# K of the next head asked for behind tiles 4 and 5 of a head in place of behind tiles 8 and 9

## The chip, the cores and the metric

The kernel runs on one core of one Trainium2 chip. A core has five engines that run side by side and meet through semaphores: TensorE (PE, matrix products; PEld is its weight load), VectorE (DVE), ScalarE (ACT), GpSimd (POOL) and SyncE (SP). SP computes nothing here: it issues DMA transfers, one after the other in the order of its program, and the transfers run on 16 DMA engines. The metric is device time in microseconds (us), from one launch of the whole kernel. Lower is better.

## The reference

A transformer block with conditioning: a modulated layer norm, attention against a cached K and V, and an MLP-like mixer. In bfloat16, cut to what matters here:

```python
x: (1, 2048, 640); k_cache, v_cache: (1, 32, 2048, 128); wq: (640, 4096); wo: (4096, 640)
h = _layernorm(x) * (1 + ca) + sa
q = (h @ wq).reshape(1, 2048, 32, 128).transpose(0, 2, 1, 3)
scores = einsum('bhqd,bhkd->bhqk', q, k_cache) * 128 ** -0.5
o = einsum('bhqk,bhkd->bhqd', softmax(scores), v_cache)
x = x + ga * (o.transpose(0, 2, 1, 3).reshape(1, 2048, 4096) @ wo)
h = _layernorm(x) * (1 + cb) + sb
x = x + gb * mixer_and_mlp(h)          # w1, w2, w3, w4
```

There are 32 heads of 128 channels, 2048 queries and 2048 keys a head. K and V of one head are 512 KB each.

## The kernel before

**Stages.** A short first stage loads x and the weights and makes the modulated layer norm. Attention follows, from some 35 us to some 1290 us. After it come the product with wo, the mixer and the MLP, to the end. The change is in attention.

**Tiles.** Attention walks over 512 steps `s`: head `h = s // 16`, tile `j = s % 16` of 128 queries. A step does this:

- TensorE makes the scores of the tile, 128 x 2048, in two halves of 1024 (`qk`, L297), from the tile of Q and the transposed K of the head. K is held in two buffers, one for even and one for odd heads.
- VectorE takes each half out of PSUM, negates and scales it into `negS` (three buffers) and reduces it to the maximum of the row (L570). GpSimd joins the two maxima (L580).
- ScalarE makes the exponential into `Pb` (L583), a ring of `RPB = 8` tiles.
- The tile of probabilities has to be transposed before it can meet V. For 14 of 16 tiles this is done by a DMA transpose, a pair of tiles at a time (`transpose`, L234), into `PTs`, a ring of `RPT = 12` tiles. Tiles 10 and 11 are transposed by TensorE in place of it (L264), and taken out of PSUM by ScalarE and VectorE (L273, L275).
- Some steps later (`PVD = 11`) TensorE multiplies the transposed tile with V (`pv`, L310). V has a column of ones beside it, so the sum of the row comes along. ScalarE takes the result out (L561), GpSimd divides by the sum (L451, L458) and stores to a scratch in DRAM by its own queue (L465).
- Between these, TensorE makes Q of the next head in pieces (L248), and ScalarE takes it out (L255).

**What sets the order.** The loops over `s` append operations to one list for each engine, and each engine works its own list in that order. `G.dma("sync", ...)` appends a transfer to SP's list. Waits are worked out from what an operation reads and writes: a transpose waits for the exponential of its second tile, an exponential waits until the transpose of eight tiles earlier has landed, since it takes its place in the ring, and the scores of a head's first tile wait for the landing of K. A wait in SP's list holds everything behind it.

**SP's list in one head.** In order: transposes of pairs (0,1), (2,3), (4,5), (6,7), (8,9); then, at `j == PVD`, which is tile 11, the loads of K and V of the next head, and in every fourth head a block of wo (640 KB, four heads' rows); then the transposes of (12,13) and (14,15). K is loaded by a DMA transpose from DRAM (`load_k`, L207), V by a plain load (`load_v`, L226), wo by a plain load (`load_wo`, L217). K of heads 0 and 1 is loaded before attention starts, so 30 loads of K are in the loop, in heads 1 to 30.

Of the kernel before, what the change touches and what calls it, by code (L numbers as in the profile page):

```python
# [115 lines left out]
def bass_adaLN_cond__mha_block_cached__mixer_s_mlp__prompt_kernel(  # L116
# [3 lines left out]
    _, H, SK, DH = A_k_cache.shape  # L120
# [17 lines left out]
    with ExitStack() as es:  # L138
# [11 lines left out]
        if True:  # L150
            with ExitStack() as es1:
# [53 lines left out]
                def load_k(h):  # L205
                    hb = h % 2
                    G.dma("sync", lambda e: e.dma_start_transpose(KTs[:, hb], A_k_cache[0, h]), ("k", hb), w=[("KT", hb)])  # L207
# [24 lines left out]
                def transpose(g, n):  # L232
                    b, t = g % RPB, g % RPT
                    G.dma("sync", lambda e: e.dma_start_transpose(  # L234
                        PTs[:, t:t + n].rearrange("p r k q -> p (r k) q"), ring[:, b:b + n].rearrange("p r s -> p (r s)")),
                        ("t", b), r=[("Pb", b + i) for i in range(n)], w=[("PT", t + i, z) for i in range(n) for z in range(2)])
# [9 lines left out]
                def q_piece(h, cc, q):  # L246
                    jb = bank(("q", h, cc))
                    G.op("tensor", lambda t: t.matmul(JB[jb], wqg[:, h // WG, q, (h % WG) * 128:(h % WG + 1) * 128], hT[:, q, cc * 512:(cc + 1) * 512],  # L248
                                                      start=(q == 0), stop=(q == KT - 1)),
                         r=[("wq", h), ("hT", cc, q)], w=[("J", jb)])  # L250
# [39 lines left out]
                def qk(s, half):  # L290
                    h, j = divmod(s, NQT)
                    hb = h % 2

                    def f(t):
                        for c2 in range(2):
                            col = half * 1024 + c2 * 512
                            ins = t.matmul(Sps[:, col:col + 512], QT[:, hb, j * 128:(j + 1) * 128],  # L297
                                           KTs[:, hb, col:col + 512], start=True, stop=True)
                        return ins
                    G.op("tensor", f, r=[("QT", hb, j // 4), ("KT", hb)],  # L300
                         w=[("S", half)] + ([("Sb", 2 * half), ("Sb", 2 * half + 1)] if s == 0 else []))
# [110 lines left out]
                def q_head0(cc):  # L412
                    for q in range(KT):
                        q_piece(0, cc, q)
                    q_evac(0, cc)
# [22 lines left out]
                def mod_rows(i):  # L438
                    n0, n1 = MROW[i]
                    bank = PO[:, (i % 2) * 512:(i % 2) * 512 + n1 - n0]  # L440

                    def f(t):
                        for k in range(KT):
                            ins = t.matmul(bank, s_bc[:, k, :], wmodr[:, k, n0:n1], start=(k == 0), stop=(k == KT - 1))
                        return ins
                    G.op("tensor", f, r=[("sbc", k) for k in range(KT)] + [("wm", 1)] + WRK, w=[("O", i % 2)])
                    G.op("scalar", lambda a: a.copy(mod_bc[:, n0:n1], bank), r=[("O", i % 2)], w=[("mod", i)])
# [79 lines left out]
                for s in range(at[-1] + LAG + 1):  # L527
                    h, j = divmod(s, NQT)
                    pvs = PVS.get(s, [])
                    evacs = []  # L530
                    if s <= 2:
                        for i in ((0,), (1, 2), range(3, len(MROW)))[s]:
                            mod_rows(i)
                    if s == 3:
                        G.op("gpsimd", lambda g: g.tensor_scalar(
                            out=mod_bc[:, 2 * D:3 * D], in0=mod_bc[:, 2 * D:3 * D], scalar1=1.0, scalar2=1.0, op0=ALU.add, op1=ALU.mult),
                            r=[("mod", i) for i in range(len(MROW))], w=["mod"])
                    for half in range(2):
                        if s < NG:
                            qk(s, half)  # L540
                        for g_ in pvs:
                            if len(pvs) == 1:
                                pv(g_, half)
                            elif g_ == pvs[half]:
                                pv(g_, 0)
                                pv(g_, 1)
                        if s == 0 and half == 1:
                            q_head0(NQC - 1)
                        if h + 1 < H and 2 * j + half in QPIECE:
                            cc, q = QPIECE[2 * j + half]  # L550
                            q_piece(h + 1, cc, q)
                            if q == KT - 1:
                                evacs.append((q_evac, h + 1, cc))
                        for r, pt in [(r, pt) for r in range(2) for pt in PE_TILES]:
                            g = s - PE_LAG[pt] - r
                            if 0 <= g < NG and g % NQT == pt:
                                t_piece(g, r, half)
                                if half == 1:
                                    evacs.append((t_evac, g, r))
                    for p in [g_ // 2 for g_ in pvs if g_ % 2 == 1]:  # L560
                        G.op("scalar", lambda a, p=p: a.copy(  # L561
                            Of[:, p % 4].rearrange("p z d -> p (z d)")[:, 0:259], PO[:, (p % 2) * 512:(p % 2) * 512 + 259]),
                            r=[("O", p % 2)], w=[("Of", p % 4)])
                    for fn, x, y in evacs:
                        if fn is q_evac or not by_dve(x, y):
                            fn(x, y)
                    for half in range(2):
                        if s < NG:
                            r8 = s % 8
                            G.op("vector", lambda v, half=half, s=s, r8=r8: v.tensor_scalar(  # L570
                                out=negS[:, s % 3, half * 1024:(half + 1) * 1024],
                                in0=Sps[:, half * 1024:(half + 1) * 1024],
                                scalar1=-SCALE, scalar2=None, op0=ALU.mult, op1=ALU.min,
                                accum_out=(nm0 if half == 0 else nm1)[:, r8:r8 + 1]),
                                r=[("S", half)], w=[("negS", s % 3), ("nmh", half, r8)])
                    for fn, x, y in evacs:
                        if fn is t_evac and by_dve(x, y):
                            fn(x, y)
                    if s < NG:
                        G.op("gpsimd", lambda g, r8=r8: g.tensor_scalar(  # L580
                            out=nm[:, r8:r8 + 1], in0=nm0[:, r8:r8 + 1], scalar1=nm1[:, r8:r8 + 1], scalar2=None, op0=ALU.min),
                            r=[("nmh", 0, r8), ("nmh", 1, r8)], w=[("nm", r8)])
                        G.op("scalar", lambda a, s=s, r8=r8: a.activation(  # L583
                            Pb[:, s % RPB, :], negS[:, s % 3, :], ACT.Exp, bias=nm[:, r8:r8 + 1], scale=-1.0),
                            r=[("negS", s % 3), ("nm", r8)], w=[("Pb", s % RPB)])
                        if not is_pe(s):
                            if s % 2 == 1 and not is_pe(s - 1):
                                transpose(s - 1, 2)
                            elif s % 2 == 1 or is_pe(s + 1):
                                transpose(s, 1)  # L590
                        if j == PVD:
                            if 1 <= h < H - 1:
                                load_k(h + 1)
                            if h < H - 1:
                                load_v(h + 1)
                            if h % WG == WG - 1:
                                load_wo(h // WG)
                    for g_ in NORMS.get(s, []):
                        gr, z = divmod(g_, 4)
                        if z == 0:  # L600
                            rcp(gr)
                        norm(gr, z)
                    if s == OT0:
                        load_ot(0)
                        for cc in range(NQC):
                            load_xt(cc)
                    if s == OT0 + 1:
                        load_ot(1)
# [247 lines left out]
```

## Time and profile before

| | |
|---|---|
| time, median of 3 runs | 1629.96 us (1628.02 to 1634.95) |
| profiled execution, its own time | 1635.84 us |
| its span, first to last instruction | 1634.0 us |
| TensorE (PE) busy | 1498.6 us, 92% |
| VectorE (DVE) busy | 1393.1 us, 85% |
| ScalarE (ACT) busy | 1295.6 us, 79% |
| GpSimd (POOL) busy | 622.8 us, 38% |
| loads of K | 32, median 4.7 us from issue to landing |
| transposes of pairs | 224, median 7.4 us from issue to landing |

The profile gives busy time of the engines, idle time and what ended it, and the rows of every instruction. For TensorE, busy time includes pipelined instructions that overlap, so a share of 92% is not 92% of its peak. SP does no work that counts as busy; its rows are the issues of transfers, and a row is as long as the issue takes, with a full queue longer than with an empty one. A row that ends in square brackets tells how long the engine sat idle before it, and whose work ended that.

### The profile page before, as it was taken

How to read it: one execution, taken by the hardware profiler on the slowest of the kernel's cores; microseconds unless marked ns; L12 is line 12 of the kernel's file. 1: busy time of each engine (PE TensorE's matmuls, PEld its weight loads, DVE VectorE, ACT ScalarE, POOL GpSimd, SP SyncE). 2: the span in 40 equal slices, each digit the busy share in tenths (PEclk: the TensorE clock that was granted, in tenths of full speed). 3: DMA queues.
4: the chain of work that ended last, by engine and by line, in shares of the span. 5: the costliest groups of instructions: out<-in, count | busy, mean ns of one | idle time of the engine just before them, and what ended most of it. 6: DMA issues, size and time to landing. Idle time of an engine off the chain costs nothing.

```text
span 1634.0 us, 34765 instructions
## 1 busy us (share of the span) xinstructions
PE 1498.6 (92%) x13978; PEld 978.8 (60%) x14231; DVE 1393.1 (85%) x2460; ACT 1295.6 (79%) x1145; POOL 622.8 (38%) x1394
## 2 busy tenths in 40 slices
PE   5899989998999899989989989999899799999998
PEld 3466666665666566666666666666666555545444
DVE  6999989998999899989999999999899346666424
ACT  4999989998999899989999999999899500045330
POOL 0144444443444344444444444444344423322000
PEclk9999999999999999999999999999999899999999
DMA  9999999999999999999999999999999995530000
GB/s 300 226 233 230 238 242 226 246 229 234 230 239 234 226 240 242 231 232 233 235 229 241 221 234 247 233 232 236 233 228 243 233 217 113 103 110 1 17 16 33
DMA packets 1151730, 333.61 MB, mean 204 GB/s; under 512 B 1127184, under 2 KB 1145552, under 8 KB 1151568
## 3 DMA queue, kind: packets, MB, share of 16 engines
q1 hardware_dynamic: 1145424, 314.58, 96.8%
q0 software_dynamic: 6144, 16.79, 3.9%
q8 instruction: 112, 1.84, 0.5%
q14 instruction: 50, 0.41, 0.1%
HBM read 43.48 MB, written 19.40 MB: 38 GB/s over the span
## 4 chain that ended last, share of the span: by engine, by line
DVE 36%; PE 25%; ACT 19%; issue 12%; DMA 7%; POOL 1%; SPq 1%; POOLq 0%
DVE negS L570 34%; ACT ring L583 13%; PE Sps L643 7%; DMA kv<-in_A_k_cache_dram 4%; PE Sps L784 4%; PE Sps L297 3%; PE PTp L310 2%; ACT Of L561 2%; PE Oaug L768 2%; PE QPp L768 2%; ACT ring L273 2%; ACT kv L255 1%; PE Sps L753 1%; DMA ring<-in_A_x_dram 1%; DVE ring L375 1%
## 5 line engine op out<-in xcount | busy, mean ns | idle before, releaser
L570 DVE TENSOR_SCALAR_CACHE_REDUCE negS<-Sps 128x1024 f32<-128x1024 f32 x1024 | 1177.8, 1219 | 54.4 <-PE Sps L297 51.9
L583 ACT ACTIVATE ring<-negS,small 128x2048 bf16<-128x2048 f32 x512 | 1023.1, 2020 | 16.6 <-POOL small L580 15.6
L310 PEld LDWEIGHTS PTp<-kv,ring 128*128 128x128 bf16 x8192 | 566.6, 99 | 249.1 <-issue 10.4
L297 PE MATMUL Sps<-kv 128*128 128x512 bf16 x1948 | 600.8, 386 | 92.4 <-DMA kv<-in_A_k_cache_dram 51.7
L310 PE MATMUL PTp<-kv,ring 128*128 128x129 bf16 x8192 | 652.5, 222 | 6.0 <-DMA ring<-ring 4.2
L580 POOL TENSOR_SCALAR small<-small 128x1 f32<-128x1 f32 x512 | 145.9, 285 | 654.6 <-DVE negS L570 654.5
L297 PEld LDWEIGHTS Sps<-kv 128*128 128x128 bf16 x2048 | 137.5, 98 | 208.2 <-DVE negS L570 117.8
L458 POOL TENSOR_SCALAR On<-Of,small 128x128 bf16<-128x128 f32 x512 | 189.8, 371 | 13.0
L681 ACT COPY kv<-PTp 128x640 bf16<-128x640 bf16 x32 | 22.0, 692 | 154.6 <-PE PTp L678 154.6
L451 POOL TENSOR_TENSOR small<-Of,small 128x4 f32<-128x4 f32 x128 | 133.1, 1040 | 5.3 <-ACT Of L561 5.2
L561 ACT COPY Of<-PTp 128x259 f32<-128x259 f32 x256 | 96.3, 376 | 40.2 <-PE PTp L310 40.2
L465 POOL DMA_DIRECT2D o_scratch<-On x128 | 103.1, 806 | 40.8 <-POOL On L458 37.2
L248 PE MATMUL Oaug<-hTx,wo 128*128 128x512 bf16 x264 | 100.4, 385 | 3.8 <-DVE hTx L407 3.7
L248 PE MATMUL QPp<-hTx,wo 128*128 128x512 bf16 x260 | 98.1, 382 | 2.7 <-ACT hTx L402 2.2
L570 DVE DVE_READ_ACCUMULATOR negS<-Sps 128x1 f32 x1024 | 84.4, 82 | 0.0
L624 POOL TENSOR_SCALAR On<-On 128x1 f32<-128x1 f32 x48 | 24.3, 507 | 153.0 <-DVE On L633 153.0
L651 DVE TENSOR_TENSOR ring<-Sps,mod_bc 128x640 f32<-128x640 f32 x16 | 13.2, 824 | 76.0 <-PE Sps L643 76.0
L643 PE MATMUL Sps<-wo,hTx 128*128 128x128 bf16 (+1 forms) x504 | 70.9, 302 | 4.7 <-DMA hTx<-o_scratch 4.4
L643 PE MATMUL Sps<-wo,negS 128*128 128x128 bf16 (+1 forms) x504 | 69.1, 298 | 2.1 <-DMA negS<-o_scratch 1.8
L788 DVE TENSOR_TENSOR ring<-Sps,ring 128x640 f32<-128x640 f32 x16 | 13.2, 824 | 66.2 <-PE Sps L784 66.2
L273 ACT COPY ring<-Oaug 128x1024 bf16<-128x1024 bf16 x64 | 64.1, 1001 | 0.0
L643 PEld LDWEIGHTS Sps<-wo,hTx 128*128 128x128 bf16 x512 | 40.0, 99 | 36.0 <-DMA hTx<-o_scratch 4.2
(82 smaller groups left out, 1013.9 us busy)
## 6 DMA issues: line engine op xcount, KB each, us to landing
kv<-in_A_v_cache_dram SPq DMA_DIRECT2D x32, 512.0 KB, 5.1
o_scratch<-On POOLq DMA_DIRECT2D x128, 128.0 KB, 4.8
ring<-in_A_x_dram SPq DMA_DIRECT2D x8, 640.0 KB, 4.9
wo<-in_A_wo_dram SPq DMA_DIRECT2D x8, 640.0 KB, 7.9
wo<-in_A_wq_dram SPq DMA_DIRECT2D x7, 640.0 KB, 8.6
ring<-ring SPq DMA_TRANSPOSE x224, 7.4
ring<-in_w_mod_dram SPq DMA_DIRECT2D x1, 3200.0 KB, 13.7
out_dram<-wo SPq DMA_DIRECT2D x16, 160.0 KB, 1.8
```

The costliest lines, as they stand in the source:

```text
L248: G.op("tensor", lambda t: t.matmul(JB[jb], wqg[:, h // WG, q, (h % WG) * 128:(h % WG + 1) * 128], hT[:, q, cc * 512:(cc + 1) * 512], star ...
L273: G.op("scalar", lambda a: a.copy(dst, src), r=[("J", jb)], w=[("PT", g % RPT, r)])
L297: ins = t.matmul(Sps[:, col:col + 512], QT[:, hb, j * 128:(j + 1) * 128], KTs[:, hb, col:col + 512], start=True, stop=True)
L310: ins = t.matmul(ob[:, 0:129], PTs[:, b, kt, :], Vaug[:, hb, kt, 0:129], start=(kt == 0), stop=(kt == NKT - 1))
L451: G.op("gpsimd", lambda g: g.tensor_tensor(out=rl[:, 4 * b:4 * b + 4], in0=Of[:].rearrange("p a z d -> p (a z) d")[:, 4 * b:4 * b + 4, 128 ...
L458: G.op("gpsimd", lambda g: g.tensor_scalar(out=On[:, b, z, :], in0=Of[:, 2 * b + z // 2, z % 2, 0:128], scalar1=rl[:, 4 * b + z:4 * b + z ...
L465: G.dma("gpsimd", lambda e: e.dma_start(o_scr[jj // 2:jj // 2 + 2, :, hh].rearrange("a p z d -> p a (z d)"), On[:, b].rearrange("p (a z) d ...
L561: G.op("scalar", lambda a, p=p: a.copy(Of[:, p % 4].rearrange("p z d -> p (z d)")[:, 0:259], PO[:, (p % 2) * 512:(p % 2) * 512 + 259]), r= ...
L570: G.op("vector", lambda v, half=half, s=s, r8=r8: v.tensor_scalar(out=negS[:, s % 3, half * 1024:(half + 1) * 1024], in0=Sps[:, half * 102 ...
L580: G.op("gpsimd", lambda g, r8=r8: g.tensor_scalar(out=nm[:, r8:r8 + 1], in0=nm0[:, r8:r8 + 1], scalar1=nm1[:, r8:r8 + 1], scalar2=None, op ...
L583: G.op("scalar", lambda a, s=s, r8=r8: a.activation(Pb[:, s % RPB, :], negS[:, s % 3, :], ACT.Exp, bias=nm[:, r8:r8 + 1], scale=-1.0), r=[ ...
L643: ins = t.matmul(YB[b][:, c0:c0 + cw], OTj[pr % 2][:, 2 * hh + z, :], wo[:, hh, c0:c0 + cw], start=(hh == 0), stop=(hh == H - 1))
```

## The change

The request for K of the next head moves up in SP's list, from behind the transposes of tiles 8 and 9 to behind those of tiles 4 and 5. It is now made at tile 5. The requests for V and for the block of wo stay at tile 11. No instruction is added or taken away.

```diff
                             elif s % 2 == 1 or is_pe(s + 1):
                                 transpose(s, 1)
+                        if j == 5 and 1 <= h < H - 1:
+                            load_k(h + 1)
                         if j == PVD:
-                            if 1 <= h < H - 1:
-                                load_k(h + 1)
                             if h < H - 1:
                                 load_v(h + 1)
                             if h % WG == WG - 1:
```

SP's list in one head is now: (0,1), (2,3), (4,5), K, (6,7), (8,9), V, in every fourth head wo, (12,13), (14,15).

## The prediction

> **What bounds the kernel now.** I read the page first, then the waits of the attention stage, then the busy time head by head, then the SP queue's rows one by one.
>
> ```profile
> span 1634.0 us, 34765 instructions
> q1 hardware_dynamic: 1145424, 314.58, 96.8%
> ```
>
> The span is 1634.0 us; the run that was profiled took 1635.84 us, 1.84 us more than its span, and stands 5.9 us (0.36%) above the median of the three runs, 1629.96. The queue that SP and the transposes use keeps the 16 DMA engines occupied for 96.8% of the span, although its traffic is thin in the last eighth.
>
> The waits between 100 and 1260 us, nearly all of attention (who waited for whom; total, times, longest):
>
> ```profile
> PE Sps L297 <- DMA kv<-in_A_k_cache_dram: 51.7, 21, 5.4
> DVE negS L570 <- PE Sps L297: 47.8, 33, 5.0
> ACT ring L583 <- POOL small L580: 10.8, 28, 1.0
> ```
>
> TensorE waits for K (L297 is the score product), and VectorE, which reduces the scores (L570), waits 47.8 us for TensorE. Nothing else stops VectorE there. Busy time for four successive heads, cut where VectorE starts a head:
>
> ```profile
> 501.32:543.60 42.28, 36.02 (x369) 24.80 (x373) 37.31 (x66) 39.91 (x33) 18.99 (x43) 0.97 1.21 234
> 543.60:582.78 39.18, 37.28 (x369) 26.16 (x375) 37.43 (x65) 35.12 (x30) 15.77 (x37) 0.95 1.17 223
> 582.78:620.01 37.23, 35.96 (x374) 24.98 (x379) 37.23 (x68) 37.20 (x32) 17.43 (x40) 1.00 1.23 247
> 620.01:657.23 37.22, 35.62 (x369) 24.16 (x374) 37.22 (x68) 37.22 (x33) 17.44 (x40) 1.00 1.17 242
> ```
>
> Columns: length, then busy PE, PEld, DVE, ACT, POOL, the clock granted, DMA share, GB/s. An undisturbed head takes 37.22 us, all of it VectorE work: that is VectorE's floor. ScalarE is as full. The first two heads lose 5.0 and 2.0 us. How a large stall looks (VectorE, then TensorE):
>
> ```profile
> 537.40 1.22 DVE L570 TENSOR_SCALAR_CACHE_REDUCE negS<-Sps 128x1024 f32<-128x1024 f32 x1
> 543.60 1.22 DVE L570 TENSOR_SCALAR_CACHE_REDUCE negS<-Sps 128x1024 f32<-128x1024 f32 x1 [4.97 <-PE Sps L297]
> 545.75 1.22 DVE L570 TENSOR_SCALAR_CACHE_REDUCE negS<-Sps 128x1024 f32<-128x1024 f32 x1 [0.92 <-PE Sps L297]
> 547.81 1.22 DVE L570 TENSOR_SCALAR_CACHE_REDUCE negS<-Sps 128x1024 f32<-128x1024 f32 x1 [0.83 <-PE Sps L297]
> 542.53 1.03 PE L297 MATMUL Sps<-kv 128*128 128x512 bf16 x2 [5.43 <-DMA kv<-in_A_k_cache_dram]
> ```
>
> 4.97 us until K lands, then 0.92 and 0.83 us more while TensorE runs below full clock (0.95 over that head) after its 5.43 us of idling. Why K is late stands in the SP queue's own rows:
>
> ```profile
> 458.61 2.35 SPq L207 DMA_TRANSPOSE kv<-in_A_k_cache_dram  x1
> 461.63 33.74 SPq L234 DMA_TRANSPOSE ring<-ring  x7
> 495.41 3.11 SPq L207 DMA_TRANSPOSE kv<-in_A_k_cache_dram  x1
> 498.57 0.58 SPq L226 DMA_DIRECT2D kv<-in_A_v_cache_dram  x1
> 499.19 1.38 SPq L217 DMA_DIRECT2D wo<-in_A_wo_dram  x1
> 500.62 37.16 SPq L234 DMA_TRANSPOSE ring<-ring  x7
> 537.82 2.29 SPq L207 DMA_TRANSPOSE kv<-in_A_k_cache_dram  x1
> 540.78 35.47 SPq L234 DMA_TRANSPOSE ring<-ring  x7
> 576.29 3.54 SPq L207 DMA_TRANSPOSE kv<-in_A_k_cache_dram  x1
> 613.92 2.02 SPq L207 DMA_TRANSPOSE kv<-in_A_k_cache_dram  x1
> ```
>
> SP issues without a break from 458.61 to 537.82: seven pair transposes (L234) of 4 to 8 us each, K, V, and every fourth head a block of wo, all in one line. K at 537.82 stands behind pair (8,9), which itself went out late because everything before it did. So the queue, not the place of K alone, is near its limit. Where SP is not behind, gaps appear between its rows; these are single rows from the one stretch of this cycle that has them:
>
> ```profile
> 546.86 4.23 SPq L234 DMA_TRANSPOSE ring<-ring  x1
> 552.62 4.04 SPq L234 DMA_TRANSPOSE ring<-ring  x1
> 557.28 4.09 SPq L234 DMA_TRANSPOSE ring<-ring  x1
> 561.88 3.89 SPq L234 DMA_TRANSPOSE ring<-ring  x1
> 566.37 5.08 SPq L234 DMA_TRANSPOSE ring<-ring  x1
> ```
>
> Each row's end to the next one's start: 552.62 - 551.09 = 1.53, then 0.62, 0.51 and 0.60, together 3.3 us, right after the large stall. (The table of SP's own waits is no help here: it names the last semaphore step before an issue ended, and an issue that is long because the queue is full looks there like a wait for ScalarE.)
>
> **The change part by part.** Thirty K loads (asked for in heads 1 to 30) move from behind pair (8,9) to behind pair (4,5); no instruction is added or removed, and the four compute engines keep their order. Only SP's order changes: K passes two pair transposes.
>
> *The stalls it removes.* K goes out two pair issues earlier. In the head above the pairs are these, and K's landing is the median over its 32 loads:
>
> ```profile
> 527.87 4.32 SPq L234 DMA_TRANSPOSE ring<-ring  x1
> 532.24 5.54 SPq L234 DMA_TRANSPOSE ring<-ring  x1
> DMA to landing us min/median/max: 4.1/4.7/14.4
> ```
>
> 537.82 - 527.87 = 9.9 us earlier, against a largest wait of 5.43. K would land near 527.9 + 4.7 = 532.6, while TensorE wanted it at 542.53 - 5.43 = 537.1. So I cost all waits for K at zero afterwards; what is removed is 47.8 us of VectorE idling, slow-clock part included.
>
> *K itself.* Its buffer was last read in the head before, so it waits for nothing. Nothing is priced for that: the cover is five tiles of 2.3 us (37.22 / 16).
>
> *The two pairs it passes.* (6,7) and (8,9) go out K's 2 to 3.5 us later. Where SP is ahead, as at 552 to 570, this is hidden by the ring of eight exponential tiles. Where SP is behind, it is not. Pair (6,7) of the head above, issued at 527.87, landed 8.4 us later, at 536.3; the exponential that reuses tile 6's buffer is the last but one of that head:
>
> ```profile
> DMA to landing us min/median/max: 8.4/8.4/8.4
> 536.55 2.01 ACT L583 ACTIVATE ring<-negS,small 128x2048 bf16<-128x2048 f32 x1
> ```
>
> Slack 0.3 us. That is what is late next: with the stall for K gone, ScalarE waits for a landing transpose, VectorE then for ScalarE.
>
> *V and wo.* They go out right after (8,9), as K no longer stands between; V's wait for TensorE lies behind work done two tiles earlier, and behind V stands only wo and pair (12,13). I cost it at zero; without that cover it would be at most K's 2 us, in a place where SP has two tiles (10, 11) without a transpose. POOL's queue, which stores the attention output, keeps its order, and K is as large as before wherever it meets those stores: zero.
>
> *The sum.* One cycle of four heads, K row to K row, is 613.92 - 458.61 = 155.3 us. VectorE needs 4 x 37.22 = 148.9, a surplus of 6.4. SP needs 155.3 - 3.3 = 152.0, if a head in which SP is ahead kept its short issues: gain 3.3. But issues are longer when the queue is full: its backlogged heads took 495.41 - 458.61 = 36.8 and, with wo, 537.82 - 495.41 = 42.4, the third 613.92 - 576.29 = 37.6; three at about 37.2 and one at 42.4 make 154.0: gain 1.3. I take the middle, 2.3 us a cycle, since the new order will have SP behind most of the time but not always. Thirty heads are 7.5 cycles: 17 us. Once only, the queue may fall behind from where it stands at 552 to where it stands at 536, which the ring absorbs, about one wo delay (42.4 - 36.8 = 5.6 us, of which part is used today): 3 us. Together 20 us. Ends kept: 7.5 x 1.3 = 10 and 47.8.
>
> The tail after attention is the same work, so 1634.0 - 20 = 1614 for the span, 1615.8 for its run, and 1629.96 - 20 = 1610 for the median.
>
> The Trainium skill, in "Perfetto Trace Analysis", section What "DMA-bound" means, counts as DMA-bound also a kernel whose issuing sequencer is solid DMA slices. By that rule alone no more than SP's gaps can be won: 7.5 x 3.3 = 25 us, 1605. The unbroken rows from 458.61 to 537.82 agree with it.
>
> **The rivals.**
>
> *A. VectorE takes all of it (48 us, 1582).* If SP's issues get shorter once no engine stalls, the attention heads run at 37.22. For it: the rows of 3.9 to 4.1 us after 552; 7 x 4.1 + 2.3 + 0.6 = 31.6 us plus other queues' traffic would fit. Against: 4.3 to 8 us whenever SP is behind, and wo's 5.6 us every fourth head. In "DMA: Bandwidth & Descriptors", section Rules for kernel authors, the Trainium skill advises to issue a DMA early and wait for it late, so that its fixed cost overlaps; that rule would give this rival, if the queue had room.
>
> *B. No change within 0.5% (1622 to 1638, about 1624).* SP is the limit throughout: stalls for K become waits for landing transposes of nearly the same length. For it: 154.0 of 155.3 us by the backlogged rows, and 96.8% on the queue. Against: the gaps of 3.3 us.
>
> *C. Slower: the pairs pay more than K did.* (6,7) and (8,9) are 2 to 3.5 us later just where the slack is 0.3 us. If ScalarE paid 2.0 us for each of the two pairs, in each of the two heads of a cycle that run backlogged, without any later wait growing shorter, that is 8 us against the surplus of 6.4 that goes: 7.5 x 1.6 = 12 us slower, 1642. It decides when the new waits exceed 6.4 us a cycle. Against it: a delay in one queue is paid once, as SP's total work is the same; and V and wo move forward by what the pairs move back.
>
> **How the numbers follow.** 0.5% of 1630 is 8 us, about what a measurement of this kernel can tell from no change. Forecast (SP-bound, 10 to 35 us won) 0.62; A (35 to 48) 0.14; B 0.16; C 0.08. Faster 0.76, same 0.16, slower 0.08. The range leaves out C, and parts of A and B: 1588 to 1625. Predicted 1610.
>
> **What would show it.** Right: no wait of TensorE for K after head 2; VectorE's idling for L297 from 47.8 to under 25 us and no longer at a head's first tile; K rows two transposes earlier, landing 9 us or so before use; new idling of ScalarE at L583, named by a transpose's landing, in the heads after a wo block; SP's rows solid, with fewer than 25 us of gaps; the granted clock at 1.00 through attention. Wrong: heads of 37.2 us throughout (A); ScalarE's new idling as large as VectorE's was (B) or larger (C); K still waited for, if SP falls more than 10 us behind.

## The result, and the profile after

The changed kernel takes 1613.57 us (median of 6 runs, 1607.07 to 1622.23) against 1630.62 us for the kernel before, measured beside it (6 runs, 1628.02 to 1637.57). The ratio is 0.989, with a 95% interval of 0.9856 to 0.9924: faster by 12 to 23 us, a little over 1%. The forecast was 1610, in a range of 1588 to 1625.

The profiled execution took 1614.36 us, its span 1612.6, 21.4 us less than before. From the page:

```profile
span 1612.6 us, 34765 instructions
q1 hardware_dynamic: 1145424, 314.58, 97.3%
L570 DVE TENSOR_SCALAR_CACHE_REDUCE negS<-Sps 128x1024 f32<-128x1024 f32 x1024 | 1177.8, 1220 | 28.8 <-ACT ring L583 15.8
L583 ACT ACTIVATE ring<-negS,small 128x2048 bf16<-128x2048 f32 x512 | 1028.3, 2046 | 30.0 <-DMA ring<-ring 25.0
```

VectorE's score reduction (L570) still sits idle for 28.8 us, but what ends most of that is now ScalarE's exponential (L583), and what ends the exponential's own idling is the landing of a transpose. The waits between 100 and 1260 us, which are the answer to those shown of before:

```profile
ACT ring L583 <- DMA ring<-ring: 25.0, 25, 2.6
DVE negS L570 <- ACT ring L583: 15.8, 20, 2.1
DVE negS L570 <- PE Sps L297: 4.5, 8, 0.9
```

No wait for K is left; it had been 51.7 us. In its place stands a wait that was not in the trace before: ScalarE for the place of a probability tile in the ring of eight. A large case (2.01 us at ScalarE, where the longest is 2.6), in the chain of waits and then at ScalarE and VectorE:

```profile
495.04 12.11 DMA ring<-ring
507.23 1.03 ACT ring L583
508.26 9.07 DMA ring<-ring
```

```profile
507.23 2.00 ACT L583 ACTIVATE ring<-negS,small 128x2048 bf16<-128x2048 f32 x1 [2.01 <-DMA ring<-ring]
509.36 1.23 DVE L570 TENSOR_SCALAR_CACHE_REDUCE negS<-Sps 128x1024 f32<-128x1024 f32 x1 [1.47 <-ACT ring L583]
```

A pair asked for at 495.04 lands 12.1 us later; the exponential that needs its place has waited 2.01 us, and VectorE then 1.47 for the exponential. SP's queue around it:

```profile
481.08 1.89 SPq L207 DMA_TRANSPOSE kv<-in_A_k_cache_dram  x1
483.02 9.77 SPq L234 DMA_TRANSPOSE ring<-ring  x2
492.83 0.72 SPq L226 DMA_DIRECT2D kv<-in_A_v_cache_dram  x1
493.59 1.40 SPq L217 DMA_DIRECT2D wo<-in_A_wo_dram  x1
495.04 27.93 SPq L234 DMA_TRANSPOSE ring<-ring  x5
523.00 1.81 SPq L207 DMA_TRANSPOSE kv<-in_A_k_cache_dram  x1
524.86 10.27 SPq L234 DMA_TRANSPOSE ring<-ring  x2
535.17 0.58 SPq L226 DMA_DIRECT2D kv<-in_A_v_cache_dram  x1
535.80 24.70 SPq L234 DMA_TRANSPOSE ring<-ring  x5
560.54 2.11 SPq L207 DMA_TRANSPOSE kv<-in_A_k_cache_dram  x1
```

K now stands between five pairs and two, and each row begins where the one before ends. (A row of x5 joins five issues and would hide gaps between them; their sum follows below.) The gaps that the kernel before had after a large stall are gone. Busy time of four heads around this place (columns as before: length; busy PE, PEld, DVE, ACT, POOL; clock; DMA share; GB/s):

```profile
491.13:531.59 40.46, 36.18 (x368) 24.29 (x372) 37.57 (x68) 37.03 (x31) 17.51 (x40) 1.00 1.20 224
531.59:572.81 41.22, 37.46 (x370) 25.80 (x375) 37.57 (x68) 39.19 (x33) 17.52 (x40) 0.96 1.25 245
572.81:610.03 37.22, 35.92 (x369) 24.16 (x374) 37.22 (x68) 37.22 (x33) 17.52 (x40) 1.00 1.27 248
610.03:647.25 37.22, 35.62 (x369) 24.17 (x374) 37.22 (x66) 37.22 (x33) 17.51 (x40) 1.00 1.20 241
```

This is the worst place of the run, and it is as bad as the place shown of before; most heads are nearer to VectorE's 37.22. For the mean, take the first and the last of the 30 requests for K in the loop. Before they stand at 108.54 and 1238.2, 29 heads apart:

```profile
108.54 2.00 SPq L207 DMA_TRANSPOSE kv<-in_A_k_cache_dram  x1
L207 SPq DMA_TRANSPOSE kv<-in_A_k_cache_dram x32: 1717/2247/12325, 8.8 to 1238.2; - x32
```

and after at 99.16 and 1207.6:

```profile
99.16 3.00 SPq L207 DMA_TRANSPOSE kv<-in_A_k_cache_dram  x1
L207 SPq DMA_TRANSPOSE kv<-in_A_k_cache_dram x32: 1487/2309/11809, 9.1 to 1207.6; - x32
```

That is 38.95 us a head before and 38.22 after. The difference, 0.73 us, times 29 is 21.2 us: all of the gain lies in attention. SP's single rows say where it comes from. Over these 29 heads the rows add up to 1092.5 us before and 1095.1 after, 2.6 more; the time between them is 37.2 us before and 13.4 after, 23.8 less, and 23.8 - 2.6 = 21.2. Of gaps longer than 0.15 us alone there were 26.8 us, and 1.8 are left. So the change took SP's idle time away and made its issues no shorter.

### The profile page after: what moved, and what is told of

Its sections match the earlier page's. It is cut to its first block, busy times and chain, and to the rows that moved or that the text cites. A ratio compares the mean times of both kernels' runs of the same rounds, so it can differ in the third digit from the quotient of the medians.

```text
span 1612.6 us, 34765 instructions
## 1 busy us (share of the span) xinstructions
PE 1491.7 (93%) x13978; PEld 959.2 (59%) x14231; DVE 1393.1 (86%) x2460; ACT 1287.8 (80%) x1145; POOL 625.5 (39%) x1394
## 4 chain that ended last, share of the span: by engine, by line
ACT 32%; DVE 21%; PE 21%; DMA 15%; issue 11%; SPq 0%; POOL 0%; ACTq 0%; DVEq 0%; POOLq 0%
ACT ring L583 24%; DVE negS L570 19%; DMA ring<-ring 12%; PE Sps L643 8%; PE Sps L784 4%; ACT Of L561 3%; ACT ring L273 2%; ACT kv L255 2%; PE Oaug L768 2%; PE QPp L768 2%; PE Sps L753 1%; PE Sps L297 1%; DMA ring<-in_A_x_dram 1%; PE PTp L310 1%; DMA o_scratch<-On 1%
## 5 line engine op out<-in xcount | busy, mean ns | idle before, releaser
L570 DVE TENSOR_SCALAR_CACHE_REDUCE negS<-Sps 128x1024 f32<-128x1024 f32 x1024 | 1177.8, 1220 | 28.8 <-ACT ring L583 15.8
L583 ACT ACTIVATE ring<-negS,small 128x2048 bf16<-128x2048 f32 x512 | 1028.3, 2046 | 30.0 <-DMA ring<-ring 25.0
L310 PEld LDWEIGHTS PTp<-kv,ring 128*128 128x128 bf16 x8192 | 560.5, 98 | 246.3 <-DMA ring<-ring 9.8
L297 PEld LDWEIGHTS Sps<-kv 128*128 128x128 bf16 x2048 | 125.4, 97 | 192.4 <-DVE negS L570 160.1
L465 POOL DMA_DIRECT2D o_scratch<-On x128 | 103.1, 806 | 40.8 <-POOL On L458 37.2
L561 ACT COPY Of<-PTp 128x259 f32<-128x259 f32 x256 | 104.6, 409 | 11.2 <-PE PTp L310 11.1
L570 DVE DVE_READ_ACCUMULATOR negS<-Sps 128x1 f32 x1024 | 85.0, 83 | 0.0
L651 DVE TENSOR_TENSOR ring<-Sps,mod_bc 128x640 f32<-128x640 f32 x16 | 13.2, 825 | 80.0 <-PE Sps L643 80.0
L788 DVE TENSOR_TENSOR ring<-Sps,ring 128x640 f32<-128x640 f32 x16 | 13.2, 825 | 66.2 <-PE Sps L784 66.2
```

What stands on the lines that cost most here:

```text
L310: ins = t.matmul(ob[:, 0:129], PTs[:, b, kt, :], Vaug[:, hb, kt, 0:129], start=(kt == 0), stop=(kt == NKT - 1))
L465: G.dma("gpsimd", lambda e: e.dma_start(o_scr[jj // 2:jj // 2 + 2, :, hh].rearrange("a p z d -> p a (z d)"), On[:, b].rearrange("p (a z) d ...
L561: G.op("scalar", lambda a, p=p: a.copy(Of[:, p % 4].rearrange("p z d -> p (z d)")[:, 0:259], PO[:, (p % 2) * 512:(p % 2) * 512 + 259]), r= ...
L583: G.op("scalar", lambda a, s=s, r8=r8: a.activation(Pb[:, s % RPB, :], negS[:, s % 3, :], ACT.Exp, bias=nm[:, r8:r8 + 1], scale=-1.0), r=[ ...
```

## The experiments

Three questions were open. Is it really the transfers that hold the changed kernel above VectorE's 37.22 us, and if so the DMA engines or SP's list? What made K late? And does it matter where in the list K stands? All times are medians; the ratio is to the kernel before, run beside it on the same chip, with its 95% interval. Several chips were used, on which the kernel before took 1629.6 to 1635.3 us, so between two rows of the table the ratios compare better than the microseconds.

| kernel | us | ratio to before |
|---|---|---|
| the changed kernel | 1613.6 | 0.989 (0.9856 to 0.9924) |
| stores twice | 1656.9 | 1.0134 (1.0099 to 1.0169) |
| no K in the loop | 1585.8 | 0.970 (0.9667 to 0.9732) |
| no wo blocks, K as changed | 1594.9 | 0.9767 (0.9724 to 0.9811) |
| no wo blocks, K as before | 1599.8 | 0.9796 (0.9758 to 0.9833) |
| V from ScalarE's queue | 1627.2 | 0.996 (0.9938 to 0.9983) |
| K behind tiles 2 and 3 | 1619.0 | 0.9899 (0.9854 to 0.9943) |
| K behind tiles 6 and 7 | 1617.2 | 0.9898 (0.9863 to 0.9933) |
| wo spread, K as changed | 1600.4 | 0.9799 (0.9763 to 0.9835) |
| wo spread, K as before | 1604.7 | 0.9816 (0.9791 to 0.984) |
| wo spread, K behind 6 and 7 | 1609.3 | 0.9854 (0.9825 to 0.9883) |
| wo spread, K in two halves | 1611.6 | 0.9848 (0.9807 to 0.989) |
| wo spread, behind tiles 0 and 1 | 1611.8 | 0.9884 (0.9863 to 0.9906) |

### Are the transfers the limit?

**The stores of the output issued twice**, in the changed kernel; SP's list is as it was (`o_scr2` is a second scratch that nothing reads):

```diff
+                    G.dma("gpsimd", lambda e: e.dma_start(
+                        o_scr2[jj // 2:jj // 2 + 2, :, hh].rearrange("a p z d -> p a (z d)"),
+                        On[:, b].rearrange("p (a z) d -> p a (z d)", a=2)),
+                        ("o2", b), r=[("On", b, z) for z in range(4)], w=[("os2", b)])
```

> The changed kernel with every store of the attention output issued a second time, into a second scratch that nothing reads: 128 more transfers of 128 KB from GpSimd's queue, none in SP's list. If the 16 DMA engines are the limit: the stores take 3.6% of the engines' time now, 58 us, and as much again comes on top: 1650 to 1675 us, ScalarE's waits for landing transposes several times 25 us. If SP's own list of issues is the limit: 1610 to 1625 us.

43 us more than the changed kernel, 40 by the ratios. From the waits between 100 and 1260 us of this kernel (L588 is the exponential; L585, L459 and L452 are GpSimd's), and the issues of SP's transposes (L235 here; duration in ns as min/median/max):

```profile
ACT ring L588 <- DMA ring<-ring: 51.7, 49, 2.5
ACT ring L588 <- POOL small L585: 5.5, 8, 1.4
ACT ring L588 <- POOL On L459: 3.5, 1, 3.5
ACT ring L588 <- POOL small L452: 2.0, 1, 2.0
```
```profile
L235 SPq DMA_TRANSPOSE ring<-ring x224: 3957/4812/7797, 44.3 to 1305.2; - x112
```

ScalarE's wait for transposes doubles from 25.0 us (I had expected several times as much), though nothing was added in front of a transpose in SP's list. GpSimd has these issues on top too, and ScalarE waits 11.0 us for it (1.4 in the changed kernel), but the time does not go there. SP's rows stay solid: its gaps over 0.15 us are 0.8 us in 29 heads, so SP hardly waits for anyone. And the same rows take longer: the transposes 4812 ns in the median against 4502, all of SP's rows 1136.6 us in 29 heads against 1095.1, 41.5 more. So the DMA engines are shared, and the added bytes are paid in time, inside SP's issues.

**No K in the loop:**

```diff
-                        if j == 5 and 1 <= h < H - 1:
+                        if j == 5 and h < 0:
                             load_k(h + 1)
```

> The changed kernel without the 30 loads of K in the loop (heads 2 to 31 use K of heads 0 and 1, so the output is not the reference's). Theory (transfers are the limit): they lose about 2 us a head, 60 us in all, more than the 22 us that VectorE idles: attention falls to VectorE's pace, 37.2 us a head, 1589 to 1595 us, and gaps appear between SP's rows. If something other than transfers holds the changed kernel above VectorE's pace: 1605 us or more.

1585.8 us, 28 less than the changed kernel (31 by the ratios), a little better than expected. VectorE's pace is reached, and gaps stand between SP's rows (here 2.7, and 3.4 us, after V, where SP waits for the exponential of tile 13):

```profile
501.00:538.20 37.20, 36.47 (x375) 24.12 (x373) 37.20 (x66) 37.20 (x32) 17.49 (x41) 1.00 1.12 232
```
```profile
518.26 0.58 SPq L226 DMA_DIRECT2D kv<-in_A_v_cache_dram  x1
521.58 33.24 SPq L234 DMA_TRANSPOSE ring<-ring  x7
554.86 0.58 SPq L226 DMA_DIRECT2D kv<-in_A_v_cache_dram  x1
558.80 24.05 SPq L234 DMA_TRANSPOSE ring<-ring  x5
```

So nothing but transfers holds the changed kernel above VectorE's floor. This run takes away K's bytes and its place in SP's list at once; it is the run with the stores that tells the two apart.

**V requested by ScalarE's queue:**

```diff
-                def load_v(h):
+                def load_v(h, eng="sync"):
...
-                    G.dma("sync", lambda e: e.dma_start(Vaug[:, hb, :, 0:128], A_v_cache[0, h].rearrange("(t p) d -> p t d", p=128)),
+                    G.dma(eng, lambda e: e.dma_start(Vaug[:, hb, :, 0:128], A_v_cache[0, h].rearrange("(t p) d -> p t d", p=128)),
...
-                                load_v(h + 1)
+                                load_v(h + 1, "scalar")
```

> The changed kernel with V requested by ScalarE's queue in place of SP's, at the same tile. If the time that SP's issues take is the limit: SP's list loses about 2 us a head, 60 us in all, and attention falls to ScalarE's pace with some 0.6 us more work a head, about 1600 to 1604 us. If the 16 DMA engines are the limit (they move the same bytes): no gain, 1609 to 1620 us, and SP's other issues become longer by what V's took.

1627.2 us: 14 us slower than the changed kernel (11 by the ratios), against either expectation's size, but on the side of the engines. (The first expectation takes 2 us a head off SP's list. V's row there is 0.58 us, 18 us over 31 heads and not 60; by this too the kernel should have become faster.) SP's list is shorter and its rows stay solid, since the transposes in it become longer, in the median 4668 ns against 4502:

```profile
L234 SPq DMA_TRANSPOSE ring<-ring x224: 3936/4668/9351, 44.8 to 1278.9; - x112
```
```profile
L234 SPq DMA_TRANSPOSE ring<-ring x224: 3966/4502/8157, 44.5 to 1262.1; - x112
```

The first is this kernel, the second the changed one. ScalarE's wait for transposes grows to 41.0 us. ScalarE's own work grows too, by 31 issues of 0.375 us, 11.6 us in all; but SP's gaps over 0.15 us are 1.8 us in 29 heads, so SP hardly waited for ScalarE, and there the transposes' rows grew by 43 us while those of V and wo shrank by 30. V itself lands 7.7 us after its request, in the median, where it took 5.3. That V now runs beside the transposes in place of behind them, and takes from them at a bad moment, would explain the loss; it was not shown.

### What made K late?

**No wo blocks,** in the changed kernel and in the kernel before:

```diff
-                            if h % WG == WG - 1:
-                                load_wo(h // WG)
```

> The kernel before, K still behind tiles 8 and 9, without the loads of wo blocks (output not the reference's). Theory (K came late because the queue ahead of it was late, and a wo block is what makes it late): the large stalls right after wo heads go, some 35 of the 48 us, so about 1595 us. Rival (the place behind tiles 8 and 9 is too late by itself): the waits for K stay above 30 us and the time above 1618 us.

> The changed kernel without the eight loads of wo blocks in attention (the product with wo then uses what stands in that memory, so the output is not the reference's). Theory (the one queue of SP's transfers limits attention in the changed kernel): the queue loses about 5 us of work a block, 40 us in all, more than the 22 us that VectorE still idles in attention, so attention falls to VectorE's pace: about 1592 us, ScalarE's waits for landing transposes under 5 us. Rival (the two pairs that K passes are late by K itself, whatever else is in the queue): at most 5 us faster than the changed kernel, 1608 us or more, and the waits for transposes stay above 18 us.

From the waits between 100 and 1260 us, without wo and K as before:

```profile
PE Sps L297 <- DMA kv<-in_A_k_cache_dram: 29.5, 22, 3.2
DVE negS L570 <- PE Sps L297: 13.2, 17, 2.1
```

and without wo, K as changed:

```profile
ACT ring L583 <- DMA ring<-ring: 5.7, 10, 1.4
```

With K as before, 1599.8 us: without the wo blocks, K behind tiles 8 and 9 comes nearly in time. TensorE's wait for it falls from 51.7 to 29.5 us and, what counts, VectorE's from 47.8 to 13.2. With K as changed, 1594.9 us, and ScalarE's wait for transposes falls from 25.0 to 5.7. The rivals of both fall; that of the kernel before falls by its time, as waits of 29.5 us are only just under the 30 that it named. The move of K is worth about 5 us here, with intervals that overlap, where it is worth 17 with the blocks. Leaving wo out takes away its bytes as well as the burst; the next two runs keep the bytes.

**Wo spread over the heads**, each block but the last as four loads of 160 KB (`load_woq`), one a head from the head on that asked for the block, at the same place beside V. First with K as changed:

```diff
-                            if h % WG == WG - 1:
-                                load_wo(h // WG)
+                            if h == H - 1:
+                                load_wo(h // WG)
+                            elif h >= WG - 1:
+                                load_woq((h + 1) // WG - 1, (h + 1) % WG)
```

> The changed kernel with each wo block of four heads but the last split into four loads of 160 KB, one in each of the next four heads. If the total work of the queue is the limit: no gain beyond 5 us, 1608 to 1618 us, ScalarE's waits for transposes near 25 us, only spread more evenly. If the bursts are the limit (the queue falls behind after each block and the ring of eight tiles is too short for that peak): most of the 22 us of VectorE's idling goes, about 1595 us.

1600.4 us, the fastest kernel here that does all the work. The bytes are the same, so "the total is the limit" was too simple; the burst counts. ScalarE's wait for transposes is 11.3 us. Then the same with K as before:

> K as in the kernel before, behind tiles 8 and 9, with the wo blocks split into four loads over four heads. Theory (the bursts make the queue late, and lateness makes K late): VectorE's idling for K falls from 48 to some 20 us: about 1603 to 1612 us. Rival (the place of K costs by itself): above 1620 us.

```diff
                         if j == PVD:
+                            if 1 <= h < H - 1:
+                                load_k(h + 1)
```

(in the kernel with wo spread, whose request at tile 5 is taken out). 1604.7 us, as the theory had it, and not to be told from 1600.4 by the intervals. Waits of these two between 100 and 1260 us (K as changed, K as before; L302 and L575 are the score product and its reduction in these files, L588 the exponential):

```profile
ACT ring L588 <- DMA ring<-ring: 11.3, 18, 1.4
DVE negS L575 <- PE Sps L302: 5.8, 9, 1.8
```
```profile
PE Sps L302 <- DMA kv<-in_A_k_cache_dram: 33.8, 25, 3.0
DVE negS L575 <- PE Sps L302: 16.5, 19, 2.1
```

Spreading wo alone, with K left where it was, is worth more (about 1.8%) than moving K alone (1.1%).

### Does K's place matter?

**K behind tiles 2 and 3, or 6 and 7**, with wo in whole blocks (here 7; 3 in the other):

```diff
-                        if j == 5 and 1 <= h < H - 1:
+                        if j == 7 and 1 <= h < H - 1:
                             load_k(h + 1)
```

> The changed kernel with K behind tiles 2 and 3. Theory (peaks): a third pair is pushed, (4,5), whose slack in the changed kernel was 0.1 to 2.8 us, so ScalarE's waits grow by some 5 us: 1614 to 1622 us. If only the total of the queue counts: as the changed kernel, 1610 to 1618 us. If K still came late in the changed kernel: faster than 1608 us.

> The changed kernel with K behind tiles 6 and 7 in place of 4 and 5, wo in whole blocks. Theory (what is left is paid where the lateness of the queue peaks: K's 2 to 3 us push pair (6,7) past the ring's slack): K then passes pair (8,9) alone, which had about 1 us more slack than (6,7), so part of the 25 us of ScalarE's waits goes: about 1606 us, if K still lands in time (it goes out some 4 us later). If only the total of the queue counts: 1610 to 1618 us, waits for transposes near 25 us.

Both come out at a ratio of 0.990, the same as the changed kernel within the intervals. I had thought that what is left is paid at the pairs K pushes; by that theory tile 7 would have been faster, and it was not. What differs is who waits. Behind tiles 6 and 7:

```profile
PE Sps L297 <- DMA kv<-in_A_k_cache_dram: 25.8, 16, 3.7
ACT ring L583 <- DMA ring<-ring: 19.7, 19, 2.9
```

K goes out one pair's issue later and is late again, 16 times and by up to 3.7 us; ScalarE waits less for the transposes. So the place behind tiles 4 and 5 has about one pair of margin: there K lands 4.4 us before TensorE first needs it (median of the 30 loads; 1.3 to 8.9), and a pair takes 4.9 us to issue in the mean.

**With wo spread, K behind 6 and 7, and K in two halves**; the first takes the edit above, the second this one, where `load_kh` loads 1024 keys into half of the buffer and each half of the scores waits for its own:

```diff
-                        if j == 5 and 1 <= h < H - 1:
-                            load_k(h + 1)
+                        if j in (5, 7) and 1 <= h < H - 1:
+                            load_kh(h + 1, j // 2 - 2)
```

> Wo spread over the heads and K behind tiles 6 and 7. Theory (peaks): the 11 us of waits that were left with wo spread and K behind tiles 4 and 5 shrink by half, 1593 to 1598 us. If K's place among the pairs does not matter: 1600 us.

> Wo spread over the heads, and K in two halves of 1024 keys, one behind tiles 4 and 5, one behind 6 and 7. If K's 2 to 3 us as one lump cause the waits that are left with wo spread (11 us): 1592 to 1596 us. If only the amount of transfers counts: 1598 to 1604 us, as with K in one piece.

1609.3 and 1611.6 us: both slower than the 1600.4 with K whole behind 4 and 5, against every number expected. The intervals of the three ratios overlap at their ends, so this is likely and not certain. With K behind 6 and 7 it waits for K again, 33.8 us. With the halves, waits for K are 8.2 us and those for transposes 23.8.

**Wo spread, but behind tiles 0 and 1**, away from V:

```diff
+                        if j == 1 and WG <= h:
+                            load_woq(h // WG - 1, h % WG)
```

> Wo spread over the heads with each 160 KB load behind tiles 0 and 1, away from V, K behind tiles 4 and 5. If a load costs the queue most where it meets V and the gap of tiles 10 and 11 (pairs (12,13) then take 6 to 8 us to issue): faster than wo spread beside V, 1592 to 1597 us. If only the amount of transfers counts, with wo in small pieces: 1598 to 1604 us. If the loads use the gap of tiles 10 and 11, in which SP has no transpose to issue, they cost more elsewhere: 1605 to 1612 us.

1611.8 us, the third case: of the two places tried, spreading wins at the one beside tiles 10 and 11, for which SP has no transpose to issue, and not at the other. Waits for transposes are 23.9 us, as with whole blocks.

**What follows.** The DMA engines are nearly full, so a head costs about what its transfers cost. The rest is a reading that is argued from these runs, not shown by one of them: a ring of eight tiles and one pause a head, at tiles 10 and 11, decide how much of a delay is made good before an engine waits. K as before used that pause, and was late. K moved out leaves it to wo and V. A whole block of wo is more than it holds, a quarter is not.

What stays open: why the same bytes, with SP's rows solid, go through in 37.7 us a head with wo spread beside V, and in 38.2 or 38.3 with whole blocks or with wo behind tiles 0 and 1. SP's rows tell where but not why: against the changed kernel, wo spread beside V takes 47.9 us less in the rows of the transposes and 34.3 more in those of wo, in 29 heads. A deeper ring of probability tiles, which would tell how much is bursts, was not tried.

## Why the prediction was right or wrong

- **What bounds the kernel: right.** VectorE's floor of 37.22 us and a queue near its limit are both borne out: no K in the loop gives 37.2 us heads, and with K in it heads cost 38.2.
- **The stalls removed: right in total, close in margin.** No wait for K is left. But "landing 9 us or so before use" was wrong: the queue runs later than before, so that K goes out late too. K asked for at 481.08, in the rows above, landed at 485.6, and TensorE first needed it at 490.2, 4.6 us after that. Over the 30 loads the median is 4.4 us, and the smallest, for K asked for at 523.00, is 1.3. Moving K back by one pair used the margin up.
- **What is late next: right.** ScalarE's wait for the ring's place, at L583, named by a landing transpose, 25.0 us. Of the eight longest of these waits six are in the first head after a block of wo, as forecast.
- **The sum: right in total, with two terms that make up for each other.** 2.3 us a cycle of four heads plus 3 once was 20 us; measured are 21.2 us in the 29 heads of the profile and 17 in the medians. The cycle was taken too small: 0.73 x 4 = 2.9 us, close to the upper end of 3.3. The term behind it was that issues are longer when the queue is full, 154.0 - 152.0 = 2.0 us a cycle; SP's rows grew by 2.6 us over all 29 heads, 0.4 a cycle. The 3 us once do not show: 7.25 cycles of 2.9 us are already the 21.2. That the total came out so near is in part luck.
- **The gaps as a bound: right.** 25 us of gaps were forecast, 26.8 measured, and 1.8 are left. The Trainium skill, in "Perfetto Trace Analysis", section What "DMA-bound" means, counts a kernel as DMA-bound also where the issuing engine's track is solid DMA slices. The changed kernel's rows of SP agree with it. The same page of the Trainium skill, section DMA Optimizations, has it that balancing DMAs across the engines that can issue them may help where descriptor generation is the bottleneck. V from ScalarE's queue made the kernel slower here, and added stores made SP's issues longer with its list unchanged; both speak for the DMA engines as the bottleneck.
- **Rival A (all 48 us) fell,** since the queue would not go faster; it takes removing 30 transfers to get there. **Rival B fell** by the gaps, forecast at 3.3 us a cycle: SP was not the limit throughout, and they are what the change won. **Rival C fell:** it needed more than 6.4 us of new waits a cycle, and ScalarE's 25.0 us are 3.3 a cycle. K behind 2 and 3, which passes three pairs, costs no more than behind 4 and 5.
- **What the prediction did not see:** that the block of wo, which it priced at 5.6 us in every fourth head, was the cause of most large stalls, and that splitting it wins more than moving K. It took the order as given and the total as fixed.
- **A step that was only half right:** "the granted clock at 1.00 through attention". It rose from 0.981 to 0.994 over the run, but one head shown above still has 0.96.

## What to carry to other kernels

When a load comes late, look first at what made its queue late: one large transfer every few heads can be the cause, and splitting it into the queue's pauses may win more than asking for the load earlier. Where the queue is nearly full, as here, moving a request inside it can move the wait to another engine. What it could win here was the gaps between the issuing engine's rows, 26.8 us, and it won 21.2 of them.

## What the runs showed of the hardware that was not expected

- A plain load issued from another engine's queue is not free of the first queue's traffic, and can cost more than in line: V from ScalarE's queue made the kernel 14 us slower (11 by the ratios), and SP's transposes took 4668 ns in the median in place of 4502.
- Traffic of another queue lengthens SP's issue rows: with the stores on GpSimd's queue doubled and SP's list unchanged, its transposes took 4812 ns to issue in place of 4502.
- Stores cost less time per byte than the mix: 16.8 MB more of them took 40 to 43 us, by estimate 390 to 420 GB/s, where attention as a whole moves 239 GB/s (last number of the row below, the changed kernel from 100 to 1240 us). A pair of tiles to be transposed, 1.05 MB, is issued in 4.1 us when SP is ahead (the row at 557.28 of the kernel before), 256 GB/s by estimate.

```profile
100.00:1240.00 1140.00, 1074.01 (x10925) 726.44 (x11128) 1117.57 (x1947) 1114.58 (x927) 524.84 (x1199) 1.00 1.21 239
```

- The rate of a full queue is not one number: by the order and the cut of the same bytes, 37.7 to 38.5 us a head (wo spread beside V; K behind tiles 2 and 3), with SP's gaps over 0.15 us under 3 us in 29 heads.
